# A scan, a long convolution and a gate on one core: the table of instruction order, engines and PSUM banks replaced by another

## The chip, the cores and the metric

The kernel runs on one core of a Trainium2 chip. The metric is the device time of one launch in microseconds. A second, profiled execution gives the traces from which every duration in this text is read. Engines are named as in the profile: PE is the matrix engine (PEld its weight loads), DVE the vector engine, ACT the scalar engine, POOL the GpSimd engine, and SP the engine whose queue issues all transfers.

## The reference

The input has 4 batches of 6272 time steps and 256 channels. A gated recurrence comes first, and its result is projected, convolved along time, gated and projected again:

```python
sig = 1.0 / (1.0 + np.exp(-f_logit))
f = lower_bound[None, None, :] + (1.0 - lower_bound[None, None, :]) * sig
i = 1.0 - f
for t in range(S):
    h = f[:, t] * h + i[:, t] * x[:, t]
    y[:, t] = h
...
proj = x @ w_proj                      # x is the recurrence's result
x1, x2, x3 = (proj[..., :D].copy(), proj[..., D:2 * D].copy(), proj[..., 2 * D:].copy())
X2 = np.fft.rfft(x2, n=S, axis=1)
H = np.fft.rfft(filter_fft, n=S, axis=0)[None, :, :]
x2_conv = np.fft.irfft(X2 * H, n=S, axis=1)
y = x1 * x2_conv * x3
return (y @ w_out).astype(np.float32)
```

## The kernel before

All work is written as 2429 small operations in a list. Each has a kind, the engines that may run it, what it reads and writes, and a function that emits its instructions. A string, `ORDER`, holds one entry for each operation: its number, the engine that runs it, and the PSUM bank at which its result begins. `Plan.emit` walks through the string and emits; nothing else decides the order. The order of the entries is therefore the order in each engine's queue, and a queue is worked off strictly in that order. Each operation also carries `cost`, `dma`, `lag` and `margin` (a constant `MARGIN = 1.0` for the loads, the spectrum loads and the stores). `emit` does not read these numbers.

The kinds of operations, with the lines under which the profile shows them:

- **Preparation, once.** 24 groups of four warm-up matmuls (`warm`, L600) depend only on a constant, and nothing depends on them. Tables are made with a sine. The filter is loaded in 13 pieces, converted (`fr`), rotated on PE (`rot`, L630), copied (`f2`), transformed in two steps (`FF1` L655, `afs` copies, `FF2` L673, `hw` copies) and stored to DRAM as the spectrum H.
- **The recurrence (`hgrn`), per batch.** 13 chunks of 512 steps, the last of 128. Each is loaded (`load`, f_logit into FL and x into XT, three buffers of each), put through a sigmoid on ACT (`sig`, L335), multiplied on POOL (`u`, L337), and transposed on PE for each half of the channels (`su`, L349). The gate is made on ACT or DVE (`f`, L362 or L364), and the scan runs on DVE (`scan`, L370). Parts of the result are copied a second time behind its end (`wrap`, on POOL, ACT or SP).
- **The convolution (`spectrum`), per batch.** P projects x2 for all steps in 13 groups (L714), and its copies are `x2`. It needs the whole recurrence of the batch. Then 16 units, four at a time, go through `F1` (L727), a copy `A`, `F2` (L790), the product with the spectrum, and `I2` (L832) with its copy `Th`. The product is made either directly from PSUM on DVE (L813, engine `MUL` in the table), or as a copy on ACT or DVE followed by a product on POOL (`pm`, L822). The spectrum of each unit is loaded from DRAM (L768).
- **The gate, per batch.** x1 and x3 come from PE (`x13`, L398). x1 is copied (`xs`, L284, L286, L289 or L291). x3 is either multiplied straight from PSUM on DVE (`MUL`, L419) or copied too and multiplied on POOL (`z`, L428).
- **The output (`phase_o`), per batch.** `I1` (L895), a product `y` on DVE (L901), the output projection `proj` (L913), a copy `o`, and a store (L925), in 13 groups.

The table mixes these over batches: the recurrence of the next batch and the output of the present one run among each other, and both mix with the gate. Batches are counted from 0 in this text, and so are chunks and groups.

Of the kernel before, what the change touches and what calls it, by code (L numbers as in the profile page):

```python
# [60 lines left out]
class Plan:  # L61
# [63 lines left out]
    "AAYAvQAeQAOYAzYAiQAnQAoQA0gA1AAfQA5gA6YA+gAqQBDgAjQBIgBNgABIACIAPIARIAQAAUIAWIA2QA/YA3AA4AATIA7SBEYBXgA8CA9CBAUB"  # L125
    "JYBCEBFWBOYBHGBBEBGGBKQBLABMIBPSBYYBQCAVYAXYBSgBTAAwUBRKAdUBZUBaEBUWBWGBVOBhgBiYBcgBdYBjQBbEBeSBgCBkABrgBsIBtUAS"
    "ABmgBnIBoWBfKBuEBwgBxIBySBvEBpOBqOBzCB5UB6MAYYAZYADgEGgB0CD6gD8AD7gB3SB+WB4KD5gAEYB/OB1YBlICAUCBECJSEIAEHgB8WB9G"
    "B7YCKKCCYD9YEegCDQCEIEJYESgETgCQUEgACHSCREAFgCOWCIKCLYCPOCSYD+QEUACMSCNCCTUCUEEfgAGgECWEqgErgCZSCaCCGgD/IEAIEDOE"
    "EOEVYEKQCXUEhYAHACeSELAAIAEOWE3gE2gCYMCbYCfCEMIEPGEQOAJACgUCcSChECiYCdCEWQCjUCkEEaWFCgAaYCpSEXIEYIEbGEcOCqCEsACW"
    "gEiUEjMEtYCmgCnQCoAFDgCrYCwSEkMCuWCxCCvGCyYEmQEnIFMgFNgCzSE4AEoIE5YC0CCsUCtEEuWGJgEZYEvOFEAFFYCFgEySFWgEzKFXgC3Q"  # L130
    "C4AEwOExYC5UC6EE0KALAE6QC7YE7AFOADAUC+WDBMFPYC/GDCYE8IE9YE+SFggE/CFhgFAKC8UC9EAKAFGWFHGDDQDEIDFgFIODHUDIEAMAE1YF"
    "BYFJSFKCFqgDJQFrgEdYEpgDKIDLYDOUFYAFZYDPEDQWDRGB2YFQQFTUF0gF1gFLKFiADSYDMSDNCDTWDUGFaSFRIC1gFUMFSIFbCDXQDgWDYAFV"
    "MFcKFjYDZUFdQANADaMDbYDhOFsAF/gFtYFkSFeAFfIDcUFlCFmKDdEF+gDVgFnWMsgMtgF2AClgDeQDfIDnUFoGDoEFpOFuSFvCDjQFwKDkAFxU"
    "M5gFyEFzMDpWDqGM4gF3YF4QF5AF6IF7SDiYDrYGAAJdWGIgJfGDuUEBYDwWF8CGBYDvEEFYDxGDyYERYF9KJeQJiRJgoGCUGFWElYJhYJkBMggM"
    "hgGGGGHOGDEGEMC2gENADsSDGgDzQD0ID3WDtCD1gD2gD4OGZUGaECVgGbSMuAGcCGfQGgAGhUGiMMiAMjYM6AGLWGdSGeKGMGGNQGOAGVUGWMM7"
    "YGPSGQKJjWJluJmYJnXGjQGkAMvYGXUDmgGYEGTQGKgGUAJpPGRSGSKDWgJoUJsVJtQJxRJqEJrYJzJJvADlgGrSGlWJyUGmOJuFJwYJ2VGsCGnQ"
    "J0EJ1YGoIGpSJ4FJ3UGqCJ5sJ6YJ7VGvgGwWJ9FGtQGuIGyGG5SG4gHVUHWEJ8WKAQKCAKBRG0uGzYGxYG1YKDBJ+uJ/YG6YG9qG+YHCUG7qHEEH"
    "LWKEYG2QHBgHGsHFYHNGG3AKFTKHDKGWKIuKKUG8YHDYKMEHTQHKgG/SHMYHOYHUAHPuHQYHHYHXUHACKLWHYEKNuKOYHIQHeSHdgHZUHJAHaEHR"
    "WHiqHjYHgqHnQHSGHbUHcMHfYHoYHrAHmgHsYHpoHqYKPTKRDIBWICGHvgHwRKQTHyJKSrH4gHhYHkUHzYHxYH0pH1YHlEIDWILgIEGH5QHtUH7o"
    "H8YH6YHuEIHSIICIFWIGGH9oH+YKTYKUUKWMKVVKZQKXFKYYH2SH3CKbIIUgIJWIMUIKOIOsINYIQEIRYMkQMlAIdgIVSImgIZCMmIH/WIXqIAGI"  # L140
    "YYIWYIPYMoUMpEMqMNEgKaTKcDIvQIwAIaYISWIfYI5gKJYIeSMwQIgKIhYITGIiqIjYIbUMxAMyIKeSIcEKdYNFgKgCM0WM1GInUIzSIrsIsYIp"
    "EIqYNQgIoYJCgI0CIkQIlAM2OKfUKjVKkSKlFKhsNGANHYI6QKmqKnYI8oI+oI/YI9YNRgIxWIyGI1UItSI2EM8WJLgMngIuCI3UI4MI7YJDQJFo"
    "M9GNASJGYNcgJEYJHAJIYM+ONBCJAUKoRKpQNSANTYKqBNCKNIWJBENJGKroKsYKtRKvBJNYNMUJMSNNENKOJOCNOMJUgKuQKyRKzWJPYKwoKxYN"
    "dgJQqNeANogK3XK4SK0BK1GNpgK2YK5HK6qJVUJRYK7YNfYJXENUQNVAK8WNWIK+GNYTNygNzgMrgNZDK9SK/CLAYLBXLCWJJQNaLLGSJZsLDHLE"
    "uLFYNqALIKJKAJaYJSTJTDLHXNgQNkVN8gNhANlFLJvLKYNbgNiILLUNrYLMSLQTLNEJYYLRXLOqNmNLSDLVUKiYLTHN9gLXEM/gJWYNsQNtALWS"
    "NvTLYqLZYN0ANwDLUYLaVLPYNuINxLJbWJcGOHgN1YLbSR8QR9RLfWLcFNnYLdqLeYLgOR+AR/BN+ALkULlMN2SN/YOGgN3CN4KN5QNXYOQgN6AN"
    "7ILhWLiGLmUNDALuSLvKNPYLpWLnELqOOIAOAQOBAOCILjgORgODUObgOagOJYLwSOEELxCLrWLsGLtgOFML4QL5ILogOKSOSANLgLzWONUOlgOk"
    "gL0OOOEOLCL6QL7AL1WL9QL8gL2GOcAMzAOPMOTYOMKL+IMCUOUWOXSOYCMDMVAgOZKU/gL/QOVGOWOMAAOdYMEUMFEMHSMIKOeQOfAOgIOhUVLg"
    "OiEM3YVMgOjMOmASBWSCXSEHSDGMJSMKCOnYOoQOpIOrWOsGOqIMBgNjAOtOVXgLygMMUMRSVYgVNAMNMMSKL3gVBAO2QPAWO8UO3IMLgO9EPBGM"
    "GgPCSPDKPEQPFIO0UO1EVZAO4SO+WOwQO5KO/OVCYOySOzCVaYOuUOvEO6WO7GMOSPGUPHEOxIMPCMWQMXIPMUMQgPKWPLOPNEMTSMUCPIQPOUMY"  # L150
    "WPPEPJIMbQMcISAYPQSPRKPbYMZGPSUPWsPUsP8gPVYPaQPeoPXYSFYPTYPyWPcAPdYPzGMVgSGSSICSHQSLTSJoPqWSNDPiUPmEPuGPYSPZCSMR"
    "SQVSRQQFgPksPnYSOpQOgPlYSSFSToPfYPgSPhCPjYPvYP0UP1ESVXSXHPsuPtYQXgP2QP3IPoSPpCP9UQBsPrYP4WSUYP5GVOYSWQSaRScBP/sQ"
    "qgQAYPwSP6WP7OQHYP+YQCYPxCSbRSdBSYoQGUQIEQJYSeYQKsQzgVDSVECQgQQhAVFKQLYQDWQQYQEGQPUQRsQYQQaAQTsQUYQ8gQkSQlCQMWQc"
    "oQbYRFgQdYQZYSfQQNGSgUQiSQSYShAQjCSkVQmWMagQnGSmNQVQQWAQrSSisSjYVHUVjgQtqQoWQpOQvCQwYSZYVkgSlQSnoSpRQeSVIEVJMQuY"
    "SrBQfCQsYQ0WQ4GQ2uQ3YQ5YRYgVPQVQAVTSVwgVvgRhgQxUVRIVUCVVKQ1YSqXSuWQyESsHStYRQUQ+YSwGRSQRREQ9WQ/uRBuRGSRTARKCQ6UR"
    "HYROQRCYQ7ERIqSoYVGYRPARLYRJYSvWSzTS1DSxuRAYRqgRDUS0XS2vVlAVmYS3YMdQMeAMfgRZSRbqRdqRcYRUWVbQREES4SSPYSyYVKgRVGRW"
# [840 lines left out]
```

## Time and profile before

| | |
|---|---|
| median of 3 runs | 459.25 us (458.88 to 459.59) |
| profiled execution | 457.45 us, of which the span is 455.6 us |
| PE busy | 439.6 us (96%) |
| DVE busy | 407.4 us (89%) |
| ACT busy | 402.3 us (88%) |
| POOL busy | 308.8 us (68%) |
| DMA | 120.74 MB, mean 265 GB/s |

A busy share is an average over the whole span. PE's is the sum of the times in which some matmul was under way, and matmuls overlap, so 96% does not mean that PE is at its peak. The profile has also a row of 40 slices of the span for each engine and for the DMA, groups of instructions by line, and a chain that is followed back from the last instruction. Busy times in a chosen stretch of the span can be read for each engine; each such line gives the stretch, its length, the busy time and count of instructions for PE, PEld, DVE, ACT and POOL, the granted clock of PE, the DMA's mean busy share and its rate.

### The profile page before, as it was taken

How to read it: one execution, taken by the hardware profiler on the slowest of the kernel's cores; microseconds unless marked ns; L12 is line 12 of the kernel's file. 1: busy time of each engine (PE TensorE's matmuls, PEld its weight loads, DVE VectorE, ACT ScalarE, POOL GpSimd, SP SyncE). 2: the span in 40 equal slices, each digit the busy share in tenths (PEclk: the TensorE clock that was granted, in tenths of full speed). 3: DMA queues.
4: the chain of work that ended last, by engine and by line, in shares of the span. 5: the costliest groups of instructions: out<-in, count | busy, mean ns of one | idle time of the engine just before them, and what ended most of it. 6: DMA issues, size and time to landing. Idle time of an engine off the chain costs nothing.

```text
span 455.6 us, 14635 instructions
## 1 busy us (share of the span) xinstructions
PE 439.6 (96%) x6009; PEld 348.4 (76%) x6009; DVE 407.4 (89%) x476; ACT 402.3 (88%) x577; POOL 308.8 (68%) x279
## 2 busy tenths in 40 slices
PE   7899999999999999999999999999999999999998
PEld 5687778677767888777668888777778896776797
DVE  8899997799999996999999977999999976989873
ACT  5899999899999987899989998999989858987563
POOL 8888973878899542788995626899994405696400
PEclk9599999999999999999999999999999999999999
DMA  8999999767898985479776896778759721765186
GB/s 326 387 371 345 378 375 361 279 187 233 299 300 282 340 300 237 169 232 374 253 264 219 285 315 272 237 250 303 261 177 317 301 95 46 248 187 185 47 321 246
DMA packets 44434, 120.74 MB, mean 265 GB/s; under 512 B 4304, under 2 KB 7632, under 8 KB 44368
## 3 DMA queue, kind: packets, MB, share of 16 engines
q1 hardware_dynamic: 44368, 119.82, 74.5%
q8 instruction: 47, 0.77, 0.7%
q14 instruction: 19, 0.16, 0.1%
HBM read 86.12 MB, written 31.98 MB: 259 GB/s over the span
## 4 chain that ended last, share of the span: by engine, by line
PE 72%; DVE 11%; ACT 9%; issue 4%; DMA 3%; POOL 1%; SPq 0%; ACTq 0%; DVEq 0%; POOLq 0%
PE PS L398 17%; PE PS L714 9%; PE PS L832 9%; PE PS L913 8%; PE PS L790 7%; DVE HA L370 7%; PE PS L727 6%; PE PS L349 6%; PE PS L895 4%; ACT fTs L362 2%; DMA X<-in_moe_filter_fft_dram 2%; PE PS L600 2%; ACT HA L284 2%; DVE ys L901 1%; ACT X L284 1%
## 5 line engine op out<-in xcount | busy, mean ns | idle before, releaser
L337 POOL TENSOR_TENSOR XT<-XT,FL 128x1024 f32<-128x1024 f32 (+1 forms) x49 | 109.9, 2247 | 55.7 <-ACT FL L335 38.5
L370 DVE TENSOR_TENSOR_SCAN HA<-fTs,HA,PS 128x512 f16<-128x512 f32 (+1 forms) x96 | 112.7, 1202 | 2.0 <-ACT fTs L362 1.1
L398 PE MATMUL PS<-HA,W 128*128 128x490 f16 (+1 forms) x416 | 100.2, 367 | 0.3 <-ACT Th L284 0.2
L822 POOL TENSOR_TENSOR PP<-HA,Hu 98x1008 f16<-98x1008 f16 x42 | 88.0, 2106 | 5.6 <-ACT HA L284 2.6
L284 ACT CAST HA<-PS 128x1024 f16<-128x1024 f32 (+1 forms) x101 | 81.2, 831 | 3.3 <-POOL PP L822 0.8
L901 DVE TENSOR_TENSOR ys<-PS,zt 128x1024 fp32r<-128x1024 f32 (+1 forms) x52 | 58.3, 1151 | 14.0 <-PE PS L895 10.3
L813 DVE TENSOR_TENSOR PP<-PS,Hu 98x1008 f16<-98x1008 f32 x54 | 63.6, 1199 | 1.5 <-PE PS L790 0.7
L362 ACT ACTIVATE fTs<-PS,nomc 128x512 f32<-128x512 f32 (+1 forms) x90 | 59.5, 680 | 4.5 <-PE PS L349 4.2
L398 PEld LDWEIGHTS <-W 128*128 128x128 f16 x416 | 35.3, 97 | 30.2 <-issue 2.9
L428 POOL TENSOR_TENSOR zt<-XS 128x490 f16<-128x490 f32 (+1 forms) x26 | 31.8, 1223 | 39.0 <-DVE ys L901 27.4
L913 PE MATMUL PS<-Wo,ys 128*128 128x256 f32 x392 | 57.5, 293 | 0.4 <-DVE ys L901 0.3
L286 ACT ACTIVATE XS<-PS 128x490 f32<-128x490 f32 (+1 forms) x88 | 51.0, 590 | 6.8 <-DVE zt L419 2.6
L832 PEld LDWEIGHTS <-PP 98*128 98x128 f16 x1024 | 49.2, 98 | 10.1 <-POOL PP L795 1.3
L284 ACT CAST Th<-PS 128x784 f16<-128x784 f32 x63 | 52.0, 828 | 3.4 <-PE PS L832 2.7
L913 PEld LDWEIGHTS PS<-Wo,ys 128*128 128x128 f32 x392 | 49.6, 188 | 4.5 <-DVE ys L901 1.2
L832 PE MATMUL PS<-VA,PP 98*128 98x98 f16 x512 | 52.1, 207 | 0.2 <-POOL PP L795 0.2
L832 PE MATMUL PS<-VB,PP 98*128 98x98 f16 x512 | 51.8, 207 | 0.0
L419 DVE TENSOR_TENSOR zt<-PS,XS 128x490 f16<-128x490 f32 (+1 forms) x78 | 49.2, 648 | 2.7 <-ACT XS L286 0.8
L335 ACT ACTIVATE FL<-FL 128x1024 f32<-128x1024 f32 (+1 forms) x49 | 49.8, 1022 | 0.6 <-DMA FL<-in_f_logit_dram 0.6
L714 PE MATMUL PS<-W,HA 128*128 128x256 f16 x392 | 44.6, 273 | 1.1 <-ACT X L284 1.1
L714 PEld LDWEIGHTS <-HA 128*128 128x128 f16 x392 | 42.9, 142 | 2.0 <-issue 1.3
L349 PE MATMUL PS<-iden,FL 64*128 64x64 f32 x736 | 41.7, 229 | 2.6 <-ACT PP L286 0.6
(119 smaller groups left out, 778.7 us busy)
## 6 DMA issues: line engine op xcount, KB each, us to landing
FL<-in_f_logit_dram SPq DMA_DIRECT2D x45, 512.0 KB, 5.3
XT<-in_x_dram SPq DMA_DIRECT2D x45, 512.0 KB, 6.2
Hu<-H SPq DMA_DIRECT2D x39, 512.0 KB, 4.6
out_dram<-osb SPq DMA_DIRECT2D x24, 512.0 KB, 4.6
out_dram<-PP SPq DMA_DIRECT2D x16, 512.0 KB, 4.8
Hl<-H SPq DMA_DIRECT2D x13, 512.0 KB, 4.7
X<-in_moe_filter_fft_dram SPq DMA_DIRECT2D x9, 512.0 KB, 7.0
out_dram<-HA SPq DMA_DIRECT2D x8, 512.0 KB, 5.7
```

The lines of the kernel that those rows point to most:

```text
L284: nc.scalar.copy(dst, src)
L337: op("u", {"POOL": 0.1 + 0.553 * nb}, lambda e, xt=xt, ft=ft: nc.gpsimd.tensor_tensor(xt, xt, ft, op=AOP.mult), r=[("ft", k)], w=[("xt", k)])
L349: nc.tensor.transpose(bank(pb)[:, at[p] + j:at[p] + hn:nb], src[ps, j, cols], iden[ps, ps])
L362: nc.scalar.activation(fT, sT, AF.Identity, scale=by, bias=1.0)
L370: nc.vector.tensor_tensor_scan(h, fT, bank(pb)[:, 512 - hn:512 + hn], init, op0=AOP.mult, op1=AOP.add),
L398: nc.tensor.matmul(PS[:, p, 0:n], W13[:, kh, js], HA[:, HB[kh] + t0:HB[kh] + t0 + n], start=(kh == 0), stop=(kh == 1))
L714: nc.tensor.matmul(pp[:, r - r0, :], column(HB[kh], q_of(r)), W2[:, kh, :], start=(kh == 0), stop=(kh == 1))
L813: nc.vector.tensor_tensor(pr, px.unsqueeze(1).broadcast_to([TB, 2, UE, 63]), hh(), op=AOP.mult)
L822: nc.gpsimd.tensor_tensor(pr, spec[:, o, :, 1:64].unsqueeze(1).broadcast_to([TB, 2, UE, 63]), hh(), op=AOP.mult)
L832: nc.tensor.matmul(PS[:, ib + o, pr * TB:(pr + 1) * TB], PP[:TB, k, o, n, 2 * pr:2 * pr + 2, :], v[:TB], start=(n == 0), stop=(n == 1))
L901: nc.vector.tensor_tensor(late["ys"][:, yk, :, 0:rn * 128], PS[:, cb:cb + 2, 0:rn * 128], late["zt"][:].rearrange("p k r m -> p k (r m)") ...
L913: nc.tensor.matmul(po[:, i, :], late["ys"][:, yk, kh, i * 128:(i + 1) * 128], Wo[:, kh, :], start=(kh == 0), stop=(kh == 1))
```

## The change

The string `ORDER` is replaced by another of the same length, for the same operations. No other character of the kernel differs. Read as a table, it changes the sequence of operations on every engine, the engine of some operations, and the PSUM banks. The counts by engine, before and after, for the kinds that differ most over all batches:

| kind | before | after |
|---|---|---|
| xs | 113 ACT, 78 MUL, 17 DVE | 118 ACT, 71 MUL, 19 DVE |
| afs | 20 ACT, 12 DVE | 26 ACT, 6 DVE |
| wrap | 26 POOL, 9 ACT, 13 SP | 31 POOL, 6 ACT, 11 SP |

The first and last lines of the diff:

```diff
 ORDER = (
-    "AAYAvQAeQAOYAzYAiQAnQAoQA0gA1AAfQA5gA6YA+gAqQBDgAjQBIgBNgABIACIAPIARIAQAAUIAWIA2QA/YA3AA4AATIA7SBEYBXgA8CA9CBAUB"
...
-    "gl8gAyQ"
+    "AAYAkQABIACIA5gA6AAOYAPIA0gBDgAbQA+gBNgAeQBIgAzYAhQBXgAyQBSgBhgAsQA1YBcgBrgA7QA9AA8ABEYBmgAlSAQAATIAUIAWIApSA2SA"
...
+    "QAfQAnQ"
 )
```

Three characters are one entry. They are the digits of a number in base 64; divided by 64 it gives the operation, the next three bits give the engine, and the last three the bank.

More of the change, by code (lines that the diff above doesn't have):

```diff
@@ L130 @@
[L130 to L144, printed above, removed]
@@ new lines @@
+    "SEiWEjOEkOCoCEsACwUCxECuSCvCEmQEnAFNgFMgEtYEoICpUGJgCqECrYE4AE5YAKAC3SCsUC4KEuWEvOCzQCtEEwOC0AClgCyYFEAFFYC+SEyU"
+    "FWgFXgEzME0MC/CE6QE7AC5WC6GC7YE8IFOAFPYE+SFhgE/KEBYFggDAUDBEDCYFAKC8WC2gC9GDJQDKADHUExYFYADIMDDWDLYFGQFJSFqgFrgF"
+    "ZYDEOAJAFHAFKKElYALAFIIFLKDOUDPEDQWDRGFiAFjYDMUDNEC1gDSYFQWFTQFROFSOFUAF0gDZSDaCE9YFVIFsAFtYCWgDXUDYEDTSDUCFaWFd"
+    "UF1gF/gDgQF+gDeSFbOFcOCGgAMAEdYDWgFeEFfMDhAFkWDbYCmgFlOFmODfCF2AF3YEpYDcQDdAFnSMtgDiYFoCFpKDnUDoEFuQFvAFwIDjWDkG"
+    "FxUM5gM4gDGgFyEFzMDwSDxCMsgF4WF7QGIgF5GF6OGAAGBYJdSJeTDpUJfCJgrEFYF8AJiSERYDqEDrYDuWJkCJjTJnSF9IDvGE1YFBYJlDJpCG"
@@ new lines @@
+    "CUDyYGFWMggMhgGGOGHOENYDsQGDEGEMDtIDzSD0CD1gD2gDFgD3WD4OGZUGKgGVSGRQGaEGWCGSAGNUGOEGfSCVgDVgGXQGYIMiAJmYGhUGLWGT"
+    "QDmgGgKGiEGbUGMGGUIM6AG4gGjSGPWGcMGdQGQGGeIJoUJsVJtWJqsMuAGkCJxXJuFJvuJzPMvYGrQGsAJySJ2TJ4DJ0qGlUGmEGnQGvgGoIGpW"
+    "GqGJ3SJ7TJ9DGwUGtQGyEJ5qJ6YGuIG0sM7YG5WGzYJwYHVSHWCG1YJ8UKAQKCAJ+sKBRKDBGxYDlgG9uG6YHLSG+YHCUKEYG7uHKgG2QHDYKFXH"
+    "NCHEEG3AKHHHBgHFYG8YKGSKKUKMEHTQHUAHGsHHYG/WHAGHMYHdgHOYKIqKJYHPqHQYHXUHYEKLSKNqHIQHJAHeWHiuHguHhYHZSHaCHRUHSEHn"
+    "QHmgHvgMjYHbSHcKHfYHpAKPXKRHKQUKUVKWFH4gHoYHroILgIBSICCHjYHkWKSsHlGHsYKTYIDQHwUH0EHysHqYIEAIUgH1YIdgH5SHtWH9qH+Y"
@@ new lines @@
+    "HuGIHUIIEHxYJ1YHzYIFQIGAH6YKOYH7qImgH8YKVWKZXKaTKbPKcrKdYH2UIJQIKIKXGH3EKYYIMWIOuMkSIQGIPYMoQNEgINYNFgJhYIRYI5gM"
+    "lCMmKMpAIVUIXEH/WIWYIAGMqIIZsIvSIwCIaYIYYJCgISWIfYITGIeQIioIgAIhYMwSMxCMyKIbUIcEM0WNRgNQgM1GInQIpAIroIsYIzUM2OI0"
+    "EIjYJLgMnYIqYJUgNGAIkSKeQKfRKgAIoYIlKI6UI+sKhBNHYKiYIxWIyGItSI1QI/YJDWIuCKjVKkSI2AI8sI3QKlFJFuKmqI4IKnYJHGJIYM8T"
+    "I7YM9DJEYNAVNBFNdgNcgKoSNIQKpXI9YM+LKqCNMSNogNSAKtUNCNNpgNJANKINTYKrHKsYKuVJGYKvEKwtNNCNOKKxYJAWJNYJMQJBGJOAJPYJ"
+    "QoJRYNUUNVENWMJ/YNYWNzgNygKyQKzSK3TNZGNaOK0AK1CJVQJXIJrYK5DK2YNeANfYNqANrYK4SK6qK8TK+DK9ULBVJJWJYYJKGLDFK/sJZoJa"
```

98 lines of the change are left out of this document (49 added, 49 removed).

## The prediction

> **What bounds the kernel now.** I read the page from the top: busy shares, slices, the chain that ended last, then a table by stage, then single lines.
>
> ```profile
> PE 439.6 (96%) x6009; PEld 348.4 (76%) x6009; DVE 407.4 (89%) x476; ACT 402.3 (88%) x577; POOL 308.8 (68%) x279
> ...
> DMA  8999999767898985479776896778759721765186
> ...
> PE 72%; DVE 11%; ACT 9%; issue 4%; DMA 3%; POOL 1%; SPq 0%; ACTq 0%; DVEq 0%; POOLq 0%
> ```
>
> No engine is the bound everywhere: PE, DVE and ACT are all near 90%, and the DMA row is at its ceiling for the first seven slices only. So the span has to be cut at its natural joints. For each batch nothing of the F stages can begin before the projection "P" (L714) is done, and P cannot begin before the batch's last scan (L370). P starts at 71.5, 167.1, 266.0 and 366.1 us. The busy times of each engine, first in the four P stretches, then between them (columns: PE, PEld, DVE, ACT, POOL; clock, DMA share, GB/s):
>
> ```profile
> 71.50:82.20 10.70, 10.16 (x90) 9.63 (x89) 8.04 (x8) 9.56 (x11) 4.74 (x3) 1.00 0.98 353
> 167.10:178.00 10.90, 10.90 (x102) 10.90 (x101) 9.26 (x9) 7.61 (x9) 4.79 (x2) 1.00 0.92 361
> 266.00:278.50 12.50, 11.98 (x109) 11.67 (x106) 7.91 (x7) 11.16 (x12) 4.75 (x2) 1.00 1.00 358
> 366.00:376.50 10.50, 10.50 (x100) 10.48 (x97) 7.90 (x7) 5.60 (x7) 0.00 (x0) 1.00 0.18 70
> 24.00:71.50 47.50, 44.74 (x591) 35.34 (x590) 46.62 (x52) 47.31 (x74) 39.73 (x43) 1.00 1.00 366
> 82.20:167.10 84.90, 83.64 (x1287) 63.13 (x1285) 80.45 (x90) 81.53 (x122) 66.12 (x52) 1.00 0.82 272
> 178.00:266.00 88.00, 85.57 (x1322) 66.23 (x1320) 83.31 (x92) 82.63 (x124) 63.67 (x51) 1.00 0.72 248
> 278.50:366.00 87.50, 86.48 (x1345) 67.05 (x1344) 83.90 (x96) 82.17 (x121) 68.25 (x53) 1.00 0.73 255
> ```
>
> In a P stretch PE works back to back and DVE has 1.6 to 4.6 us free. Between them DVE is idle 4.5, 4.7 and 3.6 us of 85 to 88, and ACT 3.4, 5.4 and 5.3: there DVE sets the length with ACT close behind, and work taken from DVE there is worth its time, work given to it inside P is worth nothing. Up to 71.5 us DVE, ACT and the DMA (share 1.00) are full together. From 432 us on the tail is projections on PE, with DVE busy about half the time.
>
> **The sum's base.** The profiled execution took 457.45 us (span 455.6 and 1.85 around it); the median of the three plain runs is 459.25. I sum differences and apply them to the median. 0.2% (0.92 us) is about what a measurement of this kernel can tell from no change.
>
> **The change, part by part.** Only the order string differs; the margin in the operation list is not read when the program is emitted. Decoded, both tables hold the same 2429 operations. PE does the same matmuls, the DMAs are the same but for two fewer 128 KB wraps on SP (13 to 11). What moves is who copies what, and when. I count DVE's operations in each stretch, cut at the first and the last P, and price them by mean durations: scan 1.27, y 1.21, A or x2 copy 1.22, z product (xs, L419) 0.66, x1/x3 copy (L291) 0.66, afs copy 0.68, f2 0.69, f 0.74, hw 1.21, Th 0.97, product from PSUM (L813) 1.20, A-half copy 0.68.
>
> - *Start to P of batch 0:* DVE 6 afs and 2 f2 fewer, 4 f (one short, 0.32) and 1 hw more: -4.1 -1.4 +2.2 +0.3 +1.2 = -1.8. ACT takes them and two x copies: +6 afs (0.60), +2 f2 (0.69), +1 fr (1.09), +2 xs (0.59), less 4 f (0.71, one 0.37), 1 hw (1.04), 1 wrap (0.61): +3.1, of which the f2 and fr, 2.5, lie before 24 us, where ACT was busy only 16.7 us of 24. With DMA and ACT as full as DVE there I count zero; the ends are -1.8 and +0.7.
> - *Between the Ps, batch 0:* A -1.22, Th +0.97, half copy -0.68, x copies -1.3, z products +4 -1 short, +2.1: -0.2.
> - *Batch 1:* A -1.2, Th +1.0, half copies +1.4, product +1.2, an x2 that had run past the last P -1.2, x copies +1.3, four z products fewer -2.6: -0.2.
> - *Batch 2:* one x2 more +1.2, a product +1.2, half copy -0.7, x copy +0.7, a short f +0.3, four z products fewer -2.6, one y moved forward into P -1.2: -1.1.
> - *After P of batch 3:* two products fewer, one half copy and some x copies in exchange: -1.2. DVE has 7.5 us idle of 55.5 there, and PE sets the tail; I take a third, -0.4, between 0 and -1.2.
> - *Inside the Ps:* DVE -1.3, +0.3, +2.7 and +3.7 (in batches 2 and 3 more x2 copies leave ACT for DVE). In the last P, 3.7 on 7.9 busy of 10.5 is 1.1 too much, yet the last two copies are ACT's in the new order, so PE's L714 may still cover it: 0, at most +1.1.
>
> Sum: 0 - 0.2 - 0.2 - 1.1 - 0.4 = -1.9 us.
>
> *Order and waits.* The order inside a stretch has no row that prices it. The loads keep their distance: placed by the earlier work of PE, DVE and ACT (an estimate), their consumers stand under 5.7 us from the earliest issue in 6 cases before and 12 after, short by 8 and 6 us in total, against a median landing of 5.3 (FL) and 6.2 (XT). Stores and spectrum loads on SP wait for the same producers. The one wait that gets closer is the sigmoid of batch 2's last, short chunk: it was behind eight ACT operations after the previous sigmoid, 6.5 us of work, and is now behind one f. Its load lands about 5.0 us after issue, ACT has some 2.8 us to do until then, so ACT may stand 2.2 us with an f, two o copies and two more f queued behind, and the scans behind those. DVE then has a y and a scan (2.5 us) in hand: I price it at 0, at most +2.2. The two batch tails, the last three groups' y, proj and o, stand in nearly the same order: 0.
>
> *Banks and the warm-up.* PSUM pairs now also begin at odd banks. The row for a bank that is reused late is PE's wait for DVE's scan, 2.6 us in 8 times over the whole span; ends -2 and +3, taken 0. In the head, four of ten warm-up groups now stand among the rotations (L630) instead of two:
>
> ```profile
> 8.00:10.00 2.00, 1.03 (x6) 0.83 (x7) 1.93 (x9) 1.22 (x3) 1.71 (x3) 1.00 1.03 418
> 10.00:12.00 2.00, 1.31 (x8) 0.78 (x7) 1.90 (x7) 2.00 (x5) 1.77 (x2) 0.82 1.03 412
> 12.00:14.00 2.00, 1.81 (x8) 1.54 (x9) 1.86 (x7) 2.00 (x5) 0.60 (x2) 0.50 1.02 408
> ```
>
> The clock (third from the right) falls to 0.50 after a stretch of half-idle PE and stays there to 21 us, while the DMA share stays at 1.02. Rotations take 415 ns in the median and 276 at best; some 21 of them are in the slow part, so a clock that stays up saves at most 2.9 us on PE, all under a DMA that is full to 71.5 us: 0. (The Trainium skill, "TensorE: Matmul & The Clock Gate", Part 1, says the clock is halved when a window of about 3.4 us counts as idle and released after such a window of work; the trace agrees with a fall after idling, and by that rule the spread warm-up could hold the clock.)
>
> *POOL* gets work: over the three middle stretches +4 z (L428, 1.23) in batch 1 and again in batch 2, some wraps (0.62) and one u (2.38), less two late products (2.11). A z product that leaves DVE costs POOL 1.23 for DVE's 0.66. DVE's own products take 1176 to 1215 ns whatever POOL does, so I price no slowing. (The Trainium skill, "Perfetto Trace Analysis", section "Optimizing Scalar/DVE Operations", warns that the two share a read port, so shifting work between them might not help; by that the relief of batches 1 and 2 would be void and the sum -0.6. The 39 ns spread speaks against it.)
>
> **Rivals.** *POOL becomes the bound* (slower). From 300 to 336 us it is busy 35.5 of 36 us:
>
> ```profile
> 300.00:336.00 36.00, 36.00 (x540) 26.18 (x537) 35.04 (x45) 34.89 (x56) 35.47 (x31) 1.00 0.79 271
> ```
>
> Batch 2 adds 4 z less a late product and a wrap, 4.9 - 2.1 - 0.6 = 2.2 us; batch 1 adds 4.9 + 1.2 + 2.4 - 2.1 = 6.4, of which 204 to 240 us has 5.3 free, leaving 1.1. If these 3.3 delay the late products, I2 (L832) waits on POOL as PE does now for 0.2 us, and the relief of batches 1 and 2 is lost too: 459.25 + 3.3 - 0.6 = 462.0. It decides for slower once 2.8 us of it reach the chain. Against it: POOL is 1% of the chain now. Chance 0.28.
>
> *The new order waits more* (slower). In-order engines pay for each copy that stands ahead of a later-ready input; if half the bank price and the whole sigmoid stall appear, 459.25 - 1.9 + 1.5 + 2.2 = 461.1. Chance 0.12.
>
> *Nothing arrives*: the stretches are set by the ring of three load buffers rather than DVE, 459.2, or every z product on POOL holds DVE for the time it was relieved of, which leaves 459.25 - 0.6 = 458.7; both within 0.2%. For it: POOL's L337 waits 11.8 us for loads. Chance 0.15.
>
> *The forecast*, DVE relieved between the Ps, holds for 0.45 (up to -4 if stage 0 and the tail give all theirs and banks gain 1): 457.4.
>
> **Numbers.** 459.25 - 1.9 = 457.4 us. The forecast's own range is 455.2 to 458.3; the slower cases reach 462, and I widen for unpriced order by about half a us on each side: 454.7 to 462.5. Faster 0.45, same 0.15, slower 0.40.
>
> **What would show it.** Right: P starts of batches 2 and 3 come 1 to 2 us earlier, DVE busy is up by about 1 us in total but down between the Ps, and free time in the last two Ps shrinks to 1 us. Wrong: "PE PS L832 <- POOL" or "L813 <- DMA Hu" among the long waits, POOL full in more than the 36 us above, ACT idle before L335 for FL by over 2 us, or P of batch 0 later than 72.5 us.

## The result, and the profile after

| | before | after |
|---|---|---|
| median of 20 runs each | 458.37 us | 461.23 us |
| lowest to highest | 456.01 to 461.18 | 459.69 to 463.51 |
| profiled execution (span) | 457.45 us (455.6) | 462.75 us (461.0) |

The ratio is 1.0066, with a 95% interval of 1.0045 to 1.0087: the changed kernel is slower by 2.9 us. The two profiled executions lie 5.3 us apart, because the one of before is 0.9 us under its median and the one of after 1.5 us over its own. What follows shows where the time goes in the traces, and takes its size from the medians.

The page of the changed kernel, the lines that answer to those shown of before (busy time of each engine; DMA in 40 slices; the chain that ended last, by engine):

```profile
PE 439.4 (95%) x6009; PEld 346.6 (75%) x6009; DVE 411.8 (89%) x476; ACT 397.7 (86%) x575; POOL 317.8 (69%) x290
...
DMA  8989998957986896379866996497868832583186
...
PE 69%; ACT 8%; DVE 8%; POOL 5%; DMA 5%; issue 4%; SPq 0%; ACTq 0%; DVEq 0%; POOLq 0%
```

The sums say little: PE as before, DVE 4.4 us more (about 1 was forecast), ACT 4.6 less, POOL 9 more. In the DMA row, slices 3 and 7 (23 to 35 and 69 to 81 us) are 8, where before all from the second to the seventh were 9, and the chain has less of PE and DVE and more of POOL and DMA. The cut that decides is by the first P matmul (L714) of each batch. Busy times from P to P, and from the last P to the end, first before, then after (stretch, its length, PE, PEld, DVE, ACT, POOL, clock, DMA share, GB/s):

```profile
71.51:167.07 95.56, 93.76 (x1374) 72.72 (x1373) 88.46 (x97) 91.05 (x132) 70.86 (x54) 1.00 0.84 281
167.07:265.99 98.92, 96.49 (x1421) 77.15 (x1418) 92.59 (x101) 90.26 (x131) 68.46 (x53) 1.00 0.74 260
265.99:366.02 100.03, 98.49 (x1453) 78.73 (x1451) 91.83 (x103) 93.36 (x132) 73.00 (x55) 1.00 0.76 268
366.02:455.56 89.54, 86.70 (x1085) 69.04 (x1082) 68.37 (x79) 63.58 (x87) 36.06 (x34) 1.00 0.49 171
```

```profile
77.91:173.04 95.13, 92.60 (x1370) 72.38 (x1368) 87.44 (x94) 90.28 (x131) 68.14 (x54) 1.00 0.84 292
173.04:271.67 98.63, 98.06 (x1435) 77.30 (x1432) 93.78 (x102) 90.59 (x130) 71.92 (x58) 1.00 0.73 257
271.67:371.54 99.87, 97.36 (x1431) 77.65 (x1429) 94.39 (x104) 89.55 (x129) 74.96 (x57) 1.00 0.74 259
371.54:460.97 89.43, 87.24 (x1090) 69.20 (x1089) 70.92 (x82) 60.36 (x83) 40.98 (x37) 1.00 0.50 177
```

The four stages are 0.43, 0.29, 0.16 and 0.11 us shorter. All the loss, and more, lies ahead of the first P: it starts at 77.91 us instead of 71.51. Two `x13` operations (four matmuls of L398 together, 0.99 us) now stand ahead of it, so a little of those 6.40 us is work brought forward. At the P of batch 1, where as many PE operations of each kind are done in both lists, the changed kernel is 5.97 us late, and it ends 5.41 us late.

Within the start there are two places. The first is the filter stage (before, then after):

```profile
10.00:22.00 12.00, 10.76 (x45) 8.46 (x44) 9.81 (x23) 9.93 (x18) 9.82 (x15) 0.57 1.00 388
22.00:30.00 8.00, 7.23 (x63) 5.78 (x64) 6.99 (x11) 7.97 (x12) 6.21 (x7) 1.00 1.03 414
30.00:34.00 4.00, 3.85 (x62) 3.33 (x60) 3.93 (x6) 4.00 (x8) 4.00 (x5) 1.00 0.92 296
```

```profile
10.00:22.00 12.00, 7.31 (x44) 5.42 (x44) 10.02 (x28) 11.49 (x20) 9.15 (x13) 1.00 0.98 381
22.00:30.00 8.00, 7.22 (x33) 6.16 (x34) 4.33 (x7) 5.33 (x8) 5.01 (x8) 0.57 1.02 410
30.00:34.00 4.00, 3.81 (x51) 2.86 (x51) 3.96 (x6) 3.90 (x6) 3.98 (x5) 1.00 0.47 177
```

The clock's column tells it. Before, the half rate lay at 11.3 to 21.5 us, under the rotations. After, those run at full rate and the half rate lies at 22.0 to 28.8 us, under the first FF1 and FF2, where DVE and ACT wait for PE (DVE 4.33 us busy of 8 instead of 6.99). The timelines of PE show the same 20 matmuls, before and after:

```profile
22.82 2.94 PE L655 MATMUL PS<-D1r,f 128*128 128x256 f32 x20 [0.77 <-ACT f L284]
```

```profile
23.33 4.63 PE L655 MATMUL PS<-D1r,f 128*128 128x256 f32 x20 [0.48 <-ACT f L284]
```

The first scan starts at 32.84 us instead of 30.24. The loads of chunk 4, the first that use a buffer again, go out at 32.83 us instead of 30.82, and the DMA, 92% busy before, is 47% busy from 30 to 34 us.

The second place is the recurrence itself. From 30 to 70 us, the trace of before has no wait on DVE or ACT at all in the list of waits. After, the two engines' waits from 30 to 74 us are these (what waited and for what: total, times, longest):

```profile
DVE HA L370 <- ACT fTs L362: 2.1, 3, 1.0
DVE Hu L291 <- PE PS L673: 2.1, 1, 2.1
DVE fTs L364 <- PE PS L349: 0.5, 1, 0.5
...
ACT FL L335 <- DMA FL<-in_f_logit_dram: 2.2, 2, 1.1
ACT XS L335 <- DMA XS<-in_f_logit_dram: 0.7, 1, 0.7
```

In batch 0 the two halves of `XS` serve as a fourth load buffer beside the three of FL and XT, hence the last line. The second line still belongs to the filter stage. ACT stands before the sigmoids of chunks 9, 10 and 11 until their loads land. Behind those sigmoids stand copies that PE waits for, behind PE's matmuls the transposes for the gate, and DVE stands before three scans. From the first scan to the P of batch 1 the old list took 136.8 us and the new one 140.2. The 5.41 us are the sum: 2.60 to the first scan, 3.37 from there to the P of batch 1, and -0.56 to the end.

### The profile page after: what moved, and what is told of

Same layout as the page of the kernel before. It is cut to its first block, busy times and chain, and to the rows that moved or that the text cites. A ratio compares the mean times of both kernels' runs of the same rounds, so it can differ in the third digit from the quotient of the medians.

```text
span 461.0 us, 14633 instructions
## 1 busy us (share of the span) xinstructions
PE 439.4 (95%) x6009; PEld 346.6 (75%) x6009; DVE 411.8 (89%) x476; ACT 397.7 (86%) x575; POOL 317.8 (69%) x290
## 4 chain that ended last, share of the span: by engine, by line
PE 69%; ACT 8%; DVE 8%; POOL 5%; DMA 5%; issue 4%; SPq 0%; ACTq 0%; DVEq 0%; POOLq 0%
PE PS L398 17%; PE PS L714 9%; PE PS L832 8%; PE PS L913 8%; PE PS L349 7%; PE PS L790 6%; PE PS L727 6%; DVE HA L370 4%; PE PS L895 4%; PE PS L655 2%; DVE ys L901 2%; DMA out_dram<-osb 2%; ACT f L284 2%; POOL XT L337 2%; POOL PP L822 2%
## 5 line engine op out<-in xcount | busy, mean ns | idle before, releaser
L398 PE MATMUL PS<-HA,W 128*128 128x490 f16 (+1 forms) x416 | 99.7, 368 | 1.5 <-ACT osb L286 1.2
L822 POOL TENSOR_TENSOR PP<-HA,Hu 98x1008 f16<-98x1008 f16 x43 | 90.3, 2109 | 3.8 <-ACT HA L284 3.6
L284 ACT CAST HA<-PS 98x512 f16<-98x512 f32 (+1 forms) x102 | 82.4, 837 | 2.9 <-PE PS L727 1.5
L813 DVE TENSOR_TENSOR PP<-PS,Hu 98x1008 f16<-98x1008 f32 x53 | 62.4, 1199 | 2.1 <-PE PS L790 1.2
L398 PEld LDWEIGHTS <-W 128*128 128x128 f16 x416 | 35.4, 97 | 32.4 <-issue 5.0
L428 POOL TENSOR_TENSOR zt<-XS 128x490 f16<-128x490 f32 (+1 forms) x33 | 40.0, 1221 | 27.5 <-DVE ys L901 22.2
L362 ACT ACTIVATE fTs<-PS,nomc 128x512 f32<-128x512 f32 (+1 forms) x85 | 56.1, 679 | 2.6 <-PE PS L349 1.1
L284 ACT CAST Th<-PS 128x784 f16<-128x784 f32 x61 | 50.1, 826 | 4.9 <-PE PS L832 4.3
L335 ACT ACTIVATE FL<-FL 128x1024 f32<-128x1024 f32 (+1 forms) x49 | 49.4, 1014 | 2.2 <-DMA FL<-in_f_logit_dram 2.2
L419 DVE TENSOR_TENSOR zt<-PS,XS 128x490 f16<-128x490 f32 (+1 forms) x71 | 45.4, 652 | 3.2 <-ACT XS L286 1.7
L349 PE MATMUL PS<-iden,FL 64*128 64x64 f32 x736 | 42.3, 230 | 3.1 <-ACT afs L284 1.4
L714 PE MATMUL PS<-W,HA 128*128 128x256 f16 x392 | 44.0, 273 | 0.6 <-ACT X L284 0.5
L714 PEld LDWEIGHTS <-HA 128*128 128x128 f16 x392 | 42.8, 142 | 1.1 <-issue 0.6
```

The source lines that it names most:

```text
L284: nc.scalar.copy(dst, src)
L349: nc.tensor.transpose(bank(pb)[:, at[p] + j:at[p] + hn:nb], src[ps, j, cols], iden[ps, ps])
L362: nc.scalar.activation(fT, sT, AF.Identity, scale=by, bias=1.0)
L398: nc.tensor.matmul(PS[:, p, 0:n], W13[:, kh, js], HA[:, HB[kh] + t0:HB[kh] + t0 + n], start=(kh == 0), stop=(kh == 1))
L714: nc.tensor.matmul(pp[:, r - r0, :], column(HB[kh], q_of(r)), W2[:, kh, :], start=(kh == 0), stop=(kh == 1))
L813: nc.vector.tensor_tensor(pr, px.unsqueeze(1).broadcast_to([TB, 2, UE, 63]), hh(), op=AOP.mult)
```

## The experiments

A kernel here is a list of entries, so a part of the change can be made by joining the two lists. In the diffs, `OLD` and `NEW` are the two tables, `OLD[:n]` the first n entries, and `NEW - p` the entries of NEW that p does not hold, in NEW's order. The first scan is entry 147 of the old and 143 of the new list; the first P is 389 and 392. Three theories stood against each other: the loss is made by the clock in the filter stage (W), by the order and waits ahead of P (M), or by the new rest (R). Every ratio is to runs of the kernel before on the same chip.

**Joins at the first P.**

```diff
-ORDER = OLD
+ORDER = OLD[:389] + (NEW - OLD[:389])   # old_head_new_rest
+ORDER = NEW[:392] + (OLD - NEW[:392])   # new_head_old_rest
```

> The old table up to the first P of batch 0, then the new table for all that is left. Theory 1 (all of the loss arises before that P: in the traces P starts 6.4 us later and the rest is 1.0 us shorter): P starts at 71 to 72 us, the rest takes 383 us, and the time is 0.5 to 1.5 us below the kernel before. Rival (the head is only where the delay shows; the new rest is itself slower, or costs more when it begins earlier): the rest takes 385 us or more and the time is no better than before.

> The new table up to the first P of batch 0, then the old table for the rest. Theory 1: P starts at 77 to 78 us, the rest takes 384 us, and the time is 3 to 6 us above the kernel before. Rival (the loss is spread): P starts near 72 us or the time is within 1 us of the kernel before.

Measured: 460.58 us, ratio 1.0061 [1.0037, 1.0085], and 465.93 us, 1.0173 [1.0147, 1.0198]. Both were slower than theory 1 had it, and the traces show why. Seven warm-up groups, which carry other numbers in the two lists, had piled up at the joint: 28 matmuls of L600, 3.22 us, from 72.4 us in the first and from 77.3 us in the second, ahead of P. The first join was made again with the groups counted through, as in all joins that follow; the second was not:

> The old table up to the first P of batch 0, the new table behind it, as in old_head_new_rest, but with the warm-up groups counted through, so that no seven of them (28 matmuls, 3.2 us in that kernel's trace, 72.4 to 75.5 us) stand ahead of P. Theory 1, the loss is made ahead of the first P and the new rest gains a little: old_head_new_rest was 2.8 us above before, less those 3.2 us: 0.4 us below before, ratio 0.998 to 1.000. Rival, the new rest is itself slower: 1.5 to 3 us above before (1.003 to 1.006).

Measured: 459.10 us, 1.0030 [1.0009, 1.0052]. That is above the range of theory 1 and at the lower end of the rival's, so this run alone leaves a part of the loss to the new rest. Its trace shows one reason at the joint. The two `x13` operations stand between the last scan and P, with nothing to hide them and 0.52 us of waiting: P starts at 72.29 us, 0.8 later than in the trace of before, although the scans ran 0.6 us earlier. Theory R is answered better by all traces of this study together, since ten of them have the old list behind P and ten the new one. From the P of batch 1 to the end the old list took 287.9 us (standard deviation 0.6), the new one 288.1 (0.8). By stage, new less old: -0.7, +0.5, -0.3 and +0.1 us, the first of them with the 0.99 us brought forward, the second with one `I1` and one `x13` more ahead of the P of batch 2. From the first P to the end all twenty lie between 381.9 and 384.7 us. What is lost ahead of P is not won back, and behind it no further loss can be seen.

**The clock.** Four groups of the warm-up taken from among the rotations; then eight added, in TensorE's idle time; then the same with the old table.

```diff
-ORDER = NEW      # warm-up groups 7 to 10 stand among the rotations
+ORDER = NEW with those four moved ahead of the first rotation   # warm_first
```
```diff
-WARM = 24
+WARM = 32        # two more groups each behind three of the last rotations, one behind two
+ORDER = NEW with the eight   # gap_fill
+ORDER = OLD with the eight   # old_gap
```
```diff
-ORDER = OLD      # eight groups ahead of the first rotation, two behind the sixth
+ORDER = OLD with the new places: six ahead, two behind the 1st, one each behind the 5th and 7th   # old_warm
```

> The new table with the four warm-up groups that stood among the filter rotations put ahead of the first rotation, as most of them are in the old table; only PE's order differs. Theory 2a (the warm-ups among the rotations keep the clock at full rate there and so move the half-rate stretch from 11-21 us, where PE waits for the filter loads anyway, to 22-29 us, under the first FF1): the half-rate stretch begins at 10 to 13 us, the first 20 FF1 matmuls take 2.9 us instead of 4.6, the first scan starts 1.5 to 2.5 us earlier than in the changed kernel (32.8), and the time falls by 1 to 2.5 us from the changed kernel's. Rival (the clock does not matter, the first scan is set by the order of the first loads, XT of chunk 0 landing 2.3 us later): the first scan stays at 32 us or later.

> The new table with eight more warm-up groups (WARM 32 for 24, four short matmuls each) put into TensorE's idle time among the last five filter rotations, 18 to 23 us; nothing else is changed. Clock theory: the half-rate stretch that lay under the first FF1 and FF2 (22.0 to 28.8 us, 20 FF1 matmuls 4.63 us for 2.94) is gone or moved ahead, the granted clock at 22 to 29 us is 1.0, and 1.5 to 2.5 us are saved: 458.7 to 459.7, ratio to before 1.001 to 1.003. Rival, the later first scan comes from the order of the copies and mX behind those FF1, whatever the clock: as the new table, 1.006 to 1.007.

> The old table with four warm-up groups among the rotations where the new one has them (two behind the first rotation, one behind the fifth, one behind the seventh), instead of two ahead of the first and two behind the sixth; nothing else. Theory (b): a half-rate stretch under the first FF1 in most runs, the first scan 1 to 1.8 us later, and 1 to 2 us above before, 1.002 to 1.0045. Theory (a): within 0.6 us of before.

> The old table with eight more warm-up groups (WARM 32) in TensorE's idle time among its last five rotations; nothing else is changed. Clock theory: the runs of before at a mean granted clock of 0.996 to 1.000 have a median of 457.3 us, those at 0.989 one of 459.5; with the clock at 0.996 or more in nearly all runs the median falls by 0.4 to 0.8 us, ratio 0.998 to 0.9995. Rival: the groups stand in the way of the rotations or the half-rate stretch comes elsewhere: 1.000 to 1.002.

Measured: warm_first 463.89 us, 1.0134 [1.0108, 1.0160], slower and not faster as its theory had it. The half rate now lay from 12.6 to 29.6 us, in one piece, the first FF1 began at 26.05 and the first scan at 34.70. gap_fill 460.25, 1.0052 [1.0032, 1.0072]: the clock stays at 1.00 from 10 us on, the 20 matmuls take 2.84 us, the first scan starts at 31.03, 1.8 us earlier than after; yet the ratio fell from 1.0066 to 1.0052 only, 0.6 us, and the intervals overlap. The groups themselves are not free: with them in the old list (old_gap) the first scan starts at 30.54 us, against 29.1 to 29.4 in the traces of rest_only and old_head_new_rest, which have the old list there, no added groups, and the full rate. old_warm 459.84, 1.0021 [0.9992, 1.0051], unclear, with runs from 455.8 us (clock 1.0) to 462.2. old_gap 457.58, 0.9996 [0.9972, 1.0020]: no difference from before.

Each run states its mean granted clock, in steps that correspond to one stretch of 3.4 us at half rate. In the 109 runs of the kernel before that were made beside these experiments, the 62 at 0.996 or 1.000 have medians of 457.4 and 457.3 us, the 20 at 0.989 one of 459.3. In the 20 of after, the 12 at 0.993 or more have 460.6, the 8 below 462.8. A straight line through them gives 2 us per 0.01 in the first kernel and 3 in the second, and accounts for a third of the variance in the first and two thirds in the second. But the clock is no large part of the difference between them. At the same mean clock, after is 2.0 us above before at 0.993 (medians of 10 and 24 runs), 3.1 at 0.989 and 2.8 at 0.996 (two runs of after only). The pair gap_fill and old_gap says the same, since nearly every run of both was at 0.996 or 1.000: 1.0052 against 0.9996, 0.56% or 2.6 us, and the intervals do not overlap. By these medians theory W explains some tenths of the 2.9 us; the intervals would allow it up to about 1.5. In the one profiled execution it explains 1.8.

Of this pair, the stretches from 46 to 70 us, gap_fill and then old_gap:

```profile
46.00:58.00 12.00, 10.26 (x141) 8.13 (x138) 11.89 (x13) 10.94 (x18) 10.63 (x12) 1.00 0.98 347
58.00:64.00 6.00, 5.10 (x84) 4.24 (x83) 5.05 (x6) 5.71 (x10) 5.10 (x6) 1.00 1.00 380
64.00:70.00 6.00, 5.45 (x90) 4.15 (x87) 5.68 (x6) 6.00 (x11) 3.17 (x4) 1.00 0.92 287
```

```profile
46.00:58.00 12.00, 11.12 (x156) 8.90 (x152) 12.00 (x13) 11.95 (x20) 11.61 (x15) 1.00 1.01 384
58.00:64.00 6.00, 5.33 (x85) 4.47 (x85) 5.89 (x8) 6.00 (x10) 4.89 (x4) 1.00 1.04 381
64.00:70.00 6.00, 5.80 (x78) 4.10 (x76) 5.87 (x6) 5.87 (x12) 4.04 (x8) 1.00 1.01 359
```

With the new list ACT is idle 1.06 us of the first stretch and DVE 0.95 of the second; with the old one each is idle 0.13 us at most in any of the three. old_gap has no wait of DVE or ACT from 30 to 70 us in its list; gap_fill has these:

```profile
DVE HA L370 <- ACT fTs L362: 0.6, 3, 0.3
DVE fTs L364 <- PE PS L349: 0.5, 1, 0.5
...
ACT FL L335 <- DMA FL<-in_f_logit_dram: 1.3, 2, 1.0
```

From the first scan to the P of batch 1 the five traces with the whole of the old order there, and no half rate, took 136.8 to 137.8 us; the six with the new order and no half rate there 138.7 to 140.2. The means are 2.3 us apart, close to the 2.6 of the pair. (One of the six is sig_later, below, with three sigmoids moved.) That is where the loss is.

It is not more work. The stretch from the first scan to the P of batch 1, old_gap and then gap_fill:

```profile
30.54:167.29 136.75, 132.24 (x1909) 103.34 (x1905) 129.20 (x139) 132.01 (x196) 106.00 (x94) 1.00 0.89 303
31.03:169.69 138.66, 131.95 (x1899) 102.75 (x1895) 128.87 (x136) 131.88 (x197) 104.58 (x94) 1.00 0.88 303
```

DVE is busy 129.20 and 128.87 us, ACT 132.01 and 131.88, so neither has more to do with the new list. The stage is 1.91 us longer, and each of them is idle by that much more.

**Single waits of the middle taken away.**

```diff
-ACT: ... sig9 hw10 f15 afs25 sig10 afs24 hw11 ...
+ACT: ... hw10 sig9 f15 afs25 afs24 hw11 sig10 ...   # sig_later, likewise sig11 behind hw12
```
```diff
-PE: ... su15 FF1_25 FF1_24 FF2_11 su16 su17 ...
+PE: ... su15 FF1_25 su16 FF1_24 FF2_11 su17 ...     # su_gap, on top of gap_fill
```

> The new table with the sigmoids of chunks 9, 10 and 11 of batch 0 each moved on ACT behind the filter copies that stood just behind it (hw 10; afs 24 and hw 11; hw 12); their POOL products keep their place on POOL. Theory 2b (ACT stands 1.1, 1.1 and 0.7 us at these sigmoids until their loads land, and the filter copies behind them hold PSUM banks, so that PE stands before FF1 and the ready transposes of chunks 8 to 10 wait up to 3.5 us): ACT's waits for FL in 50 to 70 us fall below 1 us in all, the transpose of chunk 8 starts within 1.5 us of its product's end instead of 3.5, P of batch 0 starts 1.5 to 3.5 us earlier than in the changed kernel (77.9), and the time falls as much. Rival (the delay there only carries on what the ring of buffers inherited from the first 33 us): P starts within 0.5 us of 77.9.

> gap_fill with the first transpose-sum of chunk 8 moved up on TensorE's list, ahead of the FF1 and FF2 that stand before it (one entry moved over two). If TensorE's waits for ScalarE's afs ahead of it (0.59 us in gap_fill, 1.38 in the changed kernel's trace) make VectorE idle at 58 to 64 us (0.95 us in gap_fill): 0.5 to 1 us below gap_fill, ratio 1.003 to 1.004. If VectorE only waits at the next place instead: as gap_fill, 1.0045 to 1.006.

Measured: 461.10 us, 1.0073 [1.0047, 1.0099], and 460.04, 1.0048 [1.0025, 1.0070]. Neither won anything over its base that the runs can tell; by the intervals, a gain of about 1 us is not excluded. In sig_later's trace the waits for the loads (FL and XS) shrink from 2.9 to 0.5 us, but ACT now stands 1.0 us before PP for PE, and DVE still 1.1 us before scans for fTs. P starts at 75.89 us there, 2.0 earlier than in the trace of after, as expected, of which 0.85 us is an earlier first scan; the median did not follow. So a part of the wait went to the next place.

**Pieces of the new list, each alone in the old one.** The cuts are where the two lists hold nearly the same entries, so that a joint costs little.

```diff
-ORDER = OLD
+ORDER = OLD[:147] + (NEW - OLD[:147])                  # new_from_scan0
+ORDER = NEW[:143] + (OLD - NEW[:143])                  # new_to_scan0
+ORDER = NEW[:108] + (OLD - NEW[:108])                  # new_rot
+ORDER = OLD[:106] + (NEW - OLD[:106])                  # old_rot
+ORDER = OLD up to 106, NEW up to 173, then OLD         # new_ff
+ORDER = OLD up to 172, NEW up to 247, then OLD         # new_c2_5
+ORDER = OLD up to 249, NEW up to 338, then OLD         # new_c6_10
```

> The old table up to the first scan (143 to 147 entries: filter rotations, first FF1 and FF2, first loads), the new table from there on. Theory 1, the head ahead of the first scan makes the loss (scan 2.6 us later, first FF1 matmuls at half clock): within 0.7 us of before (0.998 to 1.002). Theory 2, the stretch from the first scan to P makes it (loads, sigmoids, copies of chunks 4 to 12: lateness grew from 2.6 to 6.4 us there in the profile): 2 to 4 us above before (1.004 to 1.009).

> The new table up to the first scan, the old one from there on. Theory 1, the head makes the loss: 2 to 3 us above before (1.004 to 1.007). Theory 2, the stretch behind it makes it: 0 to 1 us above (1.000 to 1.002).

> The new table's first 108 entries (filter loads, rotations, warm-up groups, the first FF1), the old table behind them; the two lists hold the same work up to there but for two entries, so hardly a seam. Theory W, the new place of the warm-up groups and the half-rate clock it brings under FF1 and FF2 make most of the loss: 1.5 to 2.5 us above before. Theory M, the order behind it (copies, loads and sigmoids of chunks 0 to 10) makes it: at most 0.7 us above before.

> The new table's entries 106 to 173 alone (first FF1 and FF2, sigmoids, u and scans of chunks 0 and 1), the old table ahead and behind. Theory W: within 0.7 us of before. Theory M: this is one of three stretches that share 2.5 to 3 us; 0.5 to 1.5 us above before, by a later first scan (0.8 us in gap_fill's trace with the clock at full rate) and later first releases of load buffers.

> The new table's entries 173 to 247 alone (scans of chunks 2 to 5 and what lies among them), the old table ahead and behind. Theory W: within 0.7 us of before. Theory M: 0.5 to 1.5 us above before, VectorE with idle time that the old table does not have between 34 and 55 us.

> The new table's entries 247 to 338 alone (chunks 6 to 10), the old table ahead and behind. Theory W: within 0.7 us of before. Theory M: 1 to 2 us above before, with ScalarE standing before the sigmoids of chunks 9 to 11 for their loads and VectorE before a scan for fTs (1.3 and 1.5 us in gap_fill's trace).

> The old table's first 106 entries (filter loads, rotations, warm-up groups), the new table behind them: the counterpart of new_rot. If the losses of head and middle add: the head's 3.3 us (new_rot) would be gone and the time at or below before, 0.998 to 1.001. If the new order behind costs by itself what new_from_scan0 showed: 3 to 4.5 us above before, 1.006 to 1.010, with the first scan at 29 to 30.5 us and idle VectorE and ScalarE time between 46 and 70 us.

| kernel | median us | ratio to before | first scan | P of batch 0 |
|---|---|---|---|---|
| new_from_scan0 | 461.46 | 1.0089 [1.0058, 1.0121] | 30.67 | 75.36 |
| new_to_scan0 | 462.78 | 1.0125 [1.0092, 1.0158] | 32.79 | 77.36 |
| new_rot | 461.52 | 1.0072 [1.0045, 1.0099] | 33.74 | 74.82 |
| new_ff | 460.51 | 1.0050 [1.0017, 1.0083] | 32.26 | 75.40 |
| new_c2_5 | 460.13 | 1.0032 [1.0001, 1.0063] | 29.35 | 74.16 |
| new_c6_10 | 461.88 | 1.0078 [1.0050, 1.0106] | 30.40 | 74.62 |
| old_rot | 462.32 | 1.0087 [1.0059, 1.0114] | 31.85 | 76.92 |

Every piece loses by itself, 1.5 to 5.7 us by the ratios (new_c2_5 is barely clear of noise), and the pieces do not add: new_rot (+3.3) and its counterpart old_rot (+4.0) would make 7.3, and the whole change costs 2.9. Theory M had expected shares that sum to it; new_ff (2.3) and new_c6_10 (3.6) lie above their shares, and new_rot and new_to_scan0 (5.7) above what either theory gave. So a piece's loss is in part the loss of its joints, and the pieces do not say which entries cost the 2.9 us. old_rot shows such a joint in its trace. Its rotations are the old ones and end as early as in rest_only, but PE's list behind them is the new one. The timelines of PE, rest_only and then old_rot, around the first transposes (L349) of chunk 0:

```profile
26.08 1.69 PE L655 MATMUL PS<-D1r,f 128*128 128x256 f32 x12
27.70 0.46 PE L349 MATMUL PS<-iden,FL 64*128 64x64 f32 x8
```

```profile
25.36 0.74 PE L655 MATMUL PS<-D1r,f 128*128 128x256 f32 x4 [1.05 <-DVE f L289]
...
28.08 1.70 PE L655 MATMUL PS<-D1r,f 128*128 128x256 f32 x12 [0.86 <-DVE Hu L291]
30.08 0.46 PE L349 MATMUL PS<-iden,FL 64*128 64x64 f32 x8 [0.30 <-DVE afs L289]
```

The input of that transpose was ready at 27.60 us in both. In old_rot it stands behind FF1 groups that wait for DVE, which has a late filter copy and an Hu copy first. In new_rot the first scan is 3.5 us late, and from there on nothing changes: the old list behind it takes 41.1 us to P, as in before (41.3). Joint and clock are not separated there: the rotations end 1.9 us later (23.93 against 22.05), and the half rate lies at 20.4 to 27.2 us, under the first FF1. Its runs at a mean clock of 0.993 and 0.989 are still some 2 us above those of before at the same.

**The engines without the order.** In the filter stage 13 copies changed engine: 5 `fr` between ACT and POOL, 8 `f2` between ACT and DVE.

```diff
-ORDER = OLD
+ORDER = OLD with the engines of those 13 entries as in NEW           # old_act
-ORDER = NEW with the eight groups (gap_fill)
+ORDER = the same, with the engines of those 13 entries as in OLD     # back_gap
```

> The old table with the engines alone of the 13 changed copies of the filter stage (fr, f2) as the new table has them; order and warm-up places as before. Theory (a): ScalarE, 9.9 us busy of the 12 from 10 to 22 us before and 11.3 to 11.5 in the kernels with the new head, becomes the bound of the rotations; the first FF1 starts 1 to 2 us later and the kernel ends 1 to 2 us later, ratio 1.002 to 1.0045. Theory (b): within 0.6 us of before.

> gap_fill (the new table with eight more warm-up groups) with the 13 copies back on the engines of the old table. Theory (a): the first FF1 starts 1.5 us earlier than the 23.8 us of gap_fill, and the whole is 1 to 1.8 us below gap_fill's 1.0052: ratio 1.0012 to 1.003. Theory (b): as gap_fill, 1.0045 to 1.006.

Measured: 464.66 us, 1.0134 [1.0101, 1.0167], and 468.11, 1.0219 [1.0186, 1.0253]. Both directions lose, far more than the 1 to 2 us that either theory gave, so that ScalarE as the bound of the rotations is not shown. The old order with the new engines makes queues wait for one another. The 3.3 us of PE below end at 16.3 us, and the half rate follows from 16.9 to 30.5 us, so waits and clock both have a part in the loss. old_act's waits from 8 to 28 us:

```profile
DVE f L289 <- PE PS L630: 8.2, 2, 7.4
...
ACT f L284 <- DVE f L289: 4.3, 2, 3.3
...
PE PS L600 <- ACT f L284: 3.3, 1, 3.3
```

No kernel here is measurably faster than the one before.

**Still open.** Most of the new order's loss is placed, from the first scan to P, and its size at full clock is measured, to within about 1.5 us. Which of its entries make it is not: the two places tried moved the wait without shortening the stage. The banks were not changed alone, since a bank can only be kept where the order is kept.

## Why the prediction was wrong

- *Start to P of batch 0, counted as zero, with ends at -1.8 and +0.7.* This is the step that failed. It was a sum of durations moved between DVE and ACT in a stretch that the same text had found full on three units. A sum prices how much work each has. It says nothing of whether each operation finds its input ready, and from 30 to 70 us in before every one on DVE and ACT did. The sum itself was about right: between old_gap and gap_fill, up to P, DVE has 1.95 us less to do (-1.8) and ACT 2.36 more (+3.1). Yet P came 2.8 us later there: 0.5 at the first scan and 2.3 behind it, where ACT has 0.6 us more to do and 1.7 more of idle time. Between the traces of before and after it came 6.40 us later; the medians put the loss of the whole start near 2.9. Where nothing waited, another order had little to gain, and eight other arrangements of the start (the seven pieces and old_act) all lost too.
- *"The order inside a stretch has no row that prices it"; loads short of their distance in 12 cases instead of 6, priced at 0.* The count pointed the right way and the price did not. I had set it against landings of 5.3 and 6.2 us, medians over the whole span. While the DMA is full, the loads of chunks 8 to 11 took 6.1 to 8.6 us already in before, and 5.5 to 9.5 in the changed kernel. Before's list had nothing waiting for them on ACT and DVE; in the new one ACT stood 2.9 us. sig_later, which took 2.4 us of that wait away without a gain in the median, suggests that no single wait was the price.
- *Warm-up, 0: "a clock that stays up saves at most 2.9 us on PE, all under a DMA that is full to 71.5 us".* The half rate did not go away; it moved by 10 us, from under the rotations to under the first FF1, where the first scan waits for it, and the DMA fell to 47% behind that. What I left out is that its place can matter more than its length: 10.2 us under the rotations put the first scan at 30.24 us, against 29.36 at full rate with the same list (rest_only), while 6.8 us under FF1 put it at 32.84, against 31.03 at full rate (gap_fill, with its added groups). The rule cited there from the Trainium skill, "TensorE: Matmul & The Clock Gate", Part 1, agrees in its first half (the half rate from 22.0 us follows 12 us in which PE was busy 7.31), though rest_only, with 7.69 of the same 12 us, kept the full rate. Spread as it was, the warm-up of the new table did not hold the clock.
- *Between the Ps, -0.2 -0.2 -1.1, and the tail, -0.4: DVE relieved.* Over ten traces of each list, -0.7, +0.5, -0.3 and +0.1, of which the first is 0.99 us of work done earlier; nothing of -1.9 can be seen. I had read that "there DVE sets the length". The rows beside that sentence said otherwise already: between the Ps, PE is idle 1.3, 2.4 and 1.0 us, and DVE 4.5, 4.7 and 3.6. In the third stage, inside P and outside together, PE is idle 1.54 us of 100 and DVE 8.2. DVE's busy time there then rose from 91.83 to 94.39 us, and the stage took 0.16 less.
- *Inside the Ps, 0, at most +1.1*, and *batch 2's last sigmoid, 0, at most +2.2*: both zeros held. Neither stage is longer than before. In the new table 26 of the 52 x2 copies are DVE's, 20 in the old. One term of theirs was too small: the last, short x2 copy of batches 1 and 2 moves from ACT to DVE, and it had been priced by its 256 elements in each partition, 0.3 us. On DVE it took 1.34 and 1.33 us, more than a full copy of 1024 (1.24 in the mean), and on ACT it had taken 1.28 to 1.33 us in before. That is 2 of the 3.4 us by which DVE's busy time missed its forecast.
- *POOL becomes the bound, chance 0.28.* It did not. From 300 to 336 us it is busy 35.25 us (35.47 before), as this line of the changed kernel shows, and PE's weight loads wait for its late products 1.9 us in the whole span. POOL's share of the chain rose from 1% to 5%, yet no stage behind P grew. The direct products take 1199 ns in the mean in both traces, with POOL busy 9 us more, so a shared port does not show either.

```profile
300.00:336.00 36.00, 35.95 (x550) 26.33 (x549) 35.06 (x44) 34.98 (x54) 35.25 (x31) 1.00 0.83 291
```

- *The new order waits more, chance 0.12, 461.1.* The time was right to 0.2 us, and that is luck. The kind of mechanism, copies ahead of inputs that come late, is what the waits show; the place and the terms were not right. I priced it with a sigmoid of batch 2, with banks and with a relief of 1.9 us; neither the first nor the last appeared, the banks were not measured, and the runs put the loss ahead of the first P. Of the signs that I had named against the forecast, two came: P of batch 0 later than 72.5 us, and ACT idle before L335 for FL by over 2 us. Of the signs for it none did: the P starts of batches 2 and 3 came 5.7 and 5.5 us later, and DVE was busy 4.4 us more in total.

## What to carry to other kernels

Where several units are full in the same stretch and the list of waits is empty there, do not price a reordering by the work that it moves: in this kernel such a stretch lost each time, and eight of eight partial reorderings of it cost 1.5 to 6 us of 458. Cut the span at points where both kernels have the same work behind them and compare the lateness there; a delay made ahead of a rigid stage (P to the end: 383.6 us, give or take 0.8, in twenty traces of both lists) goes through to the end undiminished. And do not size a loss of 0.6% from one pair of traces, nor add up what parts of an order cost alone.

## What the runs showed of the hardware

The place of a few idle-time matmuls moves the clock of a whole stretch: with four groups moved, all six runs had a mean clock of 0.981 or 0.982 (17.1 us at half rate in the trace); with eight added, 34 of 36 runs of three kernels had 0.996 or more. Where copies on the wrong engine make PE wait, the same eight groups do not help (back_gap, 0.982 to 0.985). The half rate comes in pieces of 3.4 us (3.4, 6.8, 10.2, 13.7 and 17.1 us in the traces), and the Trainium skill, "TensorE: Matmul & The Clock Gate", Part 1, gives that as the length of a free-running window, with which these lengths agree; it also holds that the place varies from run to run, and the mean clocks of one kernel, 0.985 to 1.000, agree with that too. Its advice there not to fit to a particular number of slow matmuls, since the ramp costs under 1% of a typical span, is right for the sum and not for a difference: at 2 to 3 us per 0.01 of mean clock it is as large as what was to be measured here.

A copy out of PSUM of a quarter of the elements can take longer than the whole: the last x2 copy, 256 elements in each partition, took 1.34 and 1.33 us on DVE in the changed kernel and 1.28 to 1.33 on ACT in before, against means of 1.24 and 1.05 for the copies of 1024. The two write in other patterns; which feature of the pattern costs the time was not tried.
